# A second seven-product level inside some products of a token-mixing MLP, with the operand sums of g parked in DRAM

## Chip, cores, metric

One core of a Trainium2 chip. The metric is device microseconds (us) of one launch, the median over repeated runs. "Faster" and "slower" mean a difference of over 2%; anything nearer is called "same", with an interval given.

Names: PE is TensorE (PEld its weight loads), DVE is VectorE, ACT is ScalarE, POOL is GpSimd, SP is SyncE, which issues most DMAs here. In the code, p1 to p7 are the seven products of a pair, i1 to i7 those of an inner product, and to park a sum is to write it to DRAM for later.

## The reference, cut to what matters

```python
S, D, F = 2048, 1024, 3584
h  = x + linear_attention(layernorm(x), wqkv, wo)      # 32 heads
u  = gelu(einsum("bsd,sf->bdf", layernorm(h), w1) + b1)   # mixer 1: contracts S
y  = einsum("bdf,fs->bds", u, w2) + b2                    # mixer 2: contracts F
h2 = h + y.transpose                                      # the output, bf16
```

The attention half ends at about 235 us of the 578 us and the change leaves it as it is. The argument is about the two mixers: 2048 x 3584 x 1024 multiply-adds each.

## The kernel before

Both mixers already use one level of a seven-product scheme (Winograd's form of Strassen's). The left operand of a product (w1 or w2) is split into four blocks a11 to a22, the moving operand (h, or g = gelu(u)) into even and odd 128-row tiles (E, O) and left and right 512-column halves. Seven block products replace eight. The price is sums of operands on DVE, and results that are chained through PSUM: B starts as a copy of A after product 1, C as a copy of B after product 6.

One "pair" is two 128-row tiles of the result. A product of a pair is 8 matmuls of 512 columns in mixer 1, 14 in mixer 2:

```python
def mm(self, m, ps, start, ks=None, cols=slice(0, CW)):          # CW = 512
    lhs, mv = self.lhs[m], self.mov[m]
    for k in range(self.nk) if ks is None else ks:               # nk = 8 or 14
        nc.tensor.matmul(ps[:, cols], lhsT=lhs[:, k, :], rhs=mv(k)[:, cols], ...)

def p1(self):  self.mm(1, self.A, True);   nc.scalar.copy(self.B[:], self.A[:])     # cut
def p6(self):  self.mm(6, self.B, False);  nc.scalar.copy(self.C[:], self.B[:])     # cut

def run_pair(st, nxt, pending, cut=None):       # cut: the case without a pending pair
    st.p1(); pending.p4(); st.p5()
    nxt.asum(5)                                 # sums of w blocks for the next pair, on DVE
    st.p6(); nxt.asum(6)
    st.p2(); st.p7(cut); nxt.asum(7)
    st.p3(); nxt.asum(3)

for p in range(NFP):                            # 14 pairs of mixer 1; mixer 2 has 8
    if p + 3 < NFP:
        load_w1_pair(p + 3)                     # w1 is loaded three pairs ahead
    ...
    run_pair(cur, nxt, pend)
```

The sums of g that mixer 2 needs as moving operands (T2, T3 and T4, 14 tiles of 128 x 512 each) stay in SBUF in this kernel.

Of the kernel before, what the change touches and what calls it, by code (L numbers as in the profile page):

```python
# [8 lines left out]
P = 128  # L9
F32 = mybir.dt.float32  # L10
# [10 lines left out]
BANK = 512  # L21
# [6 lines left out]
def kernel(  # L28
# [55 lines left out]
    warm = const.tile([P, BANK], BF16)  # L84
# [41 lines left out]

    w1_tiles = {}
    w2_tiles = {}

    def load_w1_pair(p):  # L130
        w1p = w1pool.tile([P, NS, 2 * P], BF16, tag="w1p", name="w1p")
        nc.sync.dma_start(
            w1p[:],
            B_w1[:, p * 2 * P:(p + 1) * 2 * P].rearrange("(k p) f -> p k f", p=P),
        )
        w1_tiles[p] = w1p

    def load_w2_pair(p, pool):
        w2p = pool.tile([P, NF, 2 * P], BF16, tag="w2p", name="w2p")
        nc.sync.dma_start(  # L140
            w2p[:],
            B_w2[:, p * 2 * P:(p + 1) * 2 * P].rearrange("(k p) s -> p k s", p=P),
        )
        w2_tiles[p] = w2p

    def combine(e, o, t2, t3, t4):
        lo, hi = slice(0, CW), slice(CW, 2 * CW)
        sub = ALU.subtract
        nc.vector.tensor_tensor(t3, o[:, hi], e[:, hi], sub)
        nc.vector.tensor_tensor(e[:, hi], e[:, hi], e[:, lo], sub)  # L150
        nc.vector.tensor_tensor(t2, o[:, hi], e[:, hi], sub)
        if t4 is not None:
            nc.vector.tensor_tensor(t4, o[:, lo], t2, sub)
# [26 lines left out]

    class Product7:
        def __init__(self, wt, nk, mov):
            self.nk, self.mov = nk, mov
            v = wt[:].rearrange("p (k two) (h f) -> p k two h f", two=2, h=2)
            self.a11 = v[:, :, 0, 0, :]
            self.a12 = v[:, :, 1, 0, :]
            self.a21 = v[:, :, 0, 1, :]
            self.a22 = v[:, :, 1, 1, :]
            self.lhs = {1: self.a11, 2: self.a12, 4: self.a22}

        def asum(self, m):
            a, b, op = {
                5: (self.a21, self.a22, ALU.add),
                6: (self.lhs.get(5), self.a11, ALU.subtract),
                7: (self.a11, self.a21, ALU.subtract),
                3: (self.a12, self.lhs.get(6), ALU.subtract),
            }[m]
            t = sapool.tile([P, max(NSP, NFP), P], FP16, tag="sa", name="sa")[:, 0:self.nk, :]
            self.lhs[m] = t
            return nc.vector.tensor_tensor(t, a, b, op)  # L200

        def asums(self):
            return [self.asum(m) for m in (5, 6, 7, 3)]
# [15 lines left out]

        def p1(self):  # L220
            self.A = psw.tile([P, BANK], F32, tag="w", name="psA1")
            self.mm(1, self.A, True)
            self.B = psx.tile([P, BANK], F32, tag="x", name="psB1")
            nc.scalar.copy(self.B[:], self.A[:])

        def p5(self, ks=None):
            if ks is None or ks[0] == 0:
                self.E = psz.tile([P, BANK], F32, tag="z", name="psE1")
            self.mm(5, self.E, True, ks)
            if self.whole(ks):  # L230
                self.shared(self.E)

        def p6(self):
            self.mm(6, self.B, False)
            self.C = psy.tile([P, BANK], F32, tag="y", name="psC1")
            nc.scalar.copy(self.C[:], self.B[:])
# [18 lines left out]
        def p4(self):  # L255
            for a, b, ps in self.parts:
                self.mm(4, ps, False, cols=slice(a, b))
                self.evac(1, 0, ps, a, b)
            self.done()

    class Mixer1(Product7):
        def __init__(self, p):
            super().__init__(w1_tiles[p], NSP, hmov)
            self.p = p

        def shared(self, ps):
            self.e = cpool.tile([P, BANK], F32, tag="e0", name="e1")
            nc.scalar.copy(self.e[:], ps[:])
# [13 lines left out]
        def done(self):  # L282
            p = self.p
            combine(gE[:, p, :], gO[:, p, :], gT2[:, p, :], gT3[:, p, :], None)

    class Mixer2(Product7):
        def __init__(self, p):
            super().__init__(w2_tiles[p], NFP, gmov)
            self.p = p

        def prefetch(self):
            self.hr, self.ot = [], []
            for a in range(2):
                self.hr.append(outp.tile([P, D], BF16, tag=f"hr{a}", name=f"hr{a}"))
                nc.sync.dma_start(self.hr[a][:], h_dram[2 * self.p + a][:])
                self.ot.append(outp.tile([P, D], BF16, tag=f"ot{a}", name=f"ot{a}"))

        def shared(self, ps):
            self.e = []
            for sh in range(2):  # L300
                self.e.append(cpool.tile([P, BANK], F32, tag=f"e{sh}", name="e2"))
                nc.vector.tensor_tensor(self.e[sh][:], ps[:], self.hr[sh][:, CW:D], ALU.add)

        def out(self, sh, c, src, res):
            i = 2 * self.p + sh
            nc.vector.scalar_tensor_tensor(self.ot[sh][:, c], src, b2_sb[:, i:i + 1], res, ALU.add, ALU.add)
            nc.sync.dma_start(o_dram[i * P:(i + 1) * P, c], self.ot[sh][:, c])

        def evac(self, sh, dh, ps, a=0, b=CW):
            c = slice(dh * CW + a, dh * CW + b)  # L310
            self.out(sh, c, ps[:, a:b], self.hr[sh][:, c])

        def evac_shared(self, sh, ps):
            self.out(sh, slice(CW, D), ps[:], self.e[sh][:])

        def done(self):
            pass

# [12 lines left out]
    def run_pair(st, nxt, pending, cut=None):  # L331
        st.p1()
        if pending is None:
            head, last = list(range(st.nk - 1)), [st.nk - 1]
            for ks in (head, last):
                st.p5(ks)
                st.p2(ks)
        else:
            pending.p4()
            st.p5()  # L340
        if nxt is not None:
            nxt.asum(5)
        st.p6()
        if nxt is not None:
            nxt.asum(6)
        if pending is not None:
            st.p2()
        st.p7(cut)
        if nxt is not None:
            nxt.asum(7)  # L350
        st.p3()
        if nxt is not None:
            nxt.asum(3)

    with ExitStack() as actx:
# [516 lines left out]
        sapool = sactx.enter_context(tc.tile_pool(name="sapool", bufs=5, side="right"))  # L872
        w1pool = mctx.enter_context(tc.tile_pool(name="w1pool", bufs=3, side="right"))
# [9 lines left out]
        with ExitStack() as a3:  # L883
# [86 lines left out]
            for (u, j) in q_units[8:]:  # L970
                q_unit(u, j)
                if u >= 1 and j % 2 == 1:
                    i = (u - 1) * TPC + j // 2
                    attn(i)
                    if i % 2 == 1 and i // 2 < 5:
                        (load_wo if i // 2 < 2 else load_w1_pair)((0, 1, 0, 1, 2)[i // 2])
# [33 lines left out]
    gT3 = gpool.tile([P, NFP, CW], FP16, name="gT3")  # L1010
    gT2 = gpool.tile([P, NFP, CW], FP16, name="gT2")
    cpool = ctx.enter_context(tc.tile_pool(name="cpool", bufs=1))
    w2a = ctx.enter_context(tc.tile_pool(name="w2a", bufs=1))
    hmov.update(moving(hE, hO, hT2, hT3, hT4))
    pend = None
    for p in range(NFP):
        if p + 3 < NFP:
            load_w1_pair(p + 3)
        if p == NFP - 3:
            load_w2_pair(0, w2a)  # L1020
        nxt = Mixer1(p + 1) if p + 1 < NFP else Mixer2(0)
        run_pair(cur, nxt, pend)
        pend = cur
        cur = nxt
    pend.p4()
    mctx.close()

    w2b = ctx.enter_context(tc.tile_pool(name="w2b", bufs=2, side="right", reuse_waits="tile"))
    t4pool = ctx.enter_context(tc.tile_pool(name="t4pool", bufs=1, side="right", reuse_waits="tile"))
    outp = ctx.enter_context(tc.tile_pool(name="outp", bufs=2, side="right", reuse_waits="tile"))  # L1030
    load_w2_pair(1, w2b)
    load_w2_pair(2, w2b)
    gT4 = t4pool.tile([P, NFP, CW], FP16, name="gT4")
    half = NFP // 2
    for sl in (slice(0, half), slice(half, NFP)):
        nc.vector.tensor_tensor(gT4[:, sl, :], gO[:, sl, 0:CW], gT2[:, sl, :], ALU.subtract)
    gmov.update(moving(gE, gO, gT2, gT3, gT4))
    pend = None
    for p in range(NSP):
        if p + 3 < NSP:  # L1040
            load_w2_pair(p + 3, w2a if (p + 3) % 3 == 0 else w2b)
        nxt = Mixer2(p + 1) if p + 1 < NSP else None
        cur.prefetch()
        run_pair(cur, nxt, pend, None if nxt is not None else CW - P)
        pend = cur
        cur = nxt
    pend.p4()
# [30 lines left out]
```

## Time and profile before

| | before |
|---|---|
| time, median of 4 runs | 578.89 us (578.86 to 580.63) |
| span of the profiled run | 577.5 us |
| mixer 1 / mixer 2, by the timeline | 235.4 to 405.2 / 405.2 to 574.6 us |

The page of the kernel before (span; busy time of each engine and its share; granted clock in tenths in 40 slices; DMA volume; the chain of work that ended last):

```profile
span 577.5 us, 7392 instructions
...
PE 570.2 (99%) x2832; PEld 267.5 (46%) x2854; DVE 323.6 (56%) x641; ACT 234.0 (41%) x470; POOL 1.8 (0%) x8
...
PEclk9999999999999999999999999999999999999999
...
DMA packets 109827, 66.55 MB, mean 115 GB/s; under 512 B 31826, under 2 KB 101728, under 8 KB 109792
...
PE 94%; DMA 2%; ACT 2%; DVE 2%; issue 1%; SPq 0%; ACTq 0%
```

The windows of the kernel before, one in mixer 1 and two around the turn to mixer 2 (busy us of each engine with the count of instructions, then granted clock, DMA share, GB/s):

```profile
core 0: us, PE busy (x) PEld busy (x) DVE busy (x) ACT busy (x) POOL busy (x), PEclk, DMA share, GB/s
310.00:335.00 25.00, 25.00 (x117) 11.37 (x116) 10.48 (x18) 9.49 (x15) 0.00 (x0) 1.00 0.31 84
406.00:434.00 28.00, 28.00 (x131) 12.70 (x130) 15.17 (x18) 1.79 (x4) 0.00 (x0) 1.00 0.86 229
434.00:460.00 26.00, 26.00 (x122) 11.76 (x121) 10.56 (x13) 1.71 (x3) 0.00 (x0) 1.00 0.59 159
```

PE is busy for the whole of each window at full clock, so the mixers take exactly as long as their matmuls: a pair of mixer 1 takes 12.08 us (its 56 matmuls start 216 ns apart), a pair of mixer 2 takes 21.15 us. DVE and ACT have more than half of each window free. Such a kernel gains only from fewer streamed columns, and it loses one for one whatever makes PE wait.

**A measure.** "Stalls" are worked out from the trace from 228 us on: the time between the starts of two consecutive matmuls, less N/2.4 + 2.5 ns for N columns, counted where it is over 60 ns. The formula is from the Trainium skill, "TensorE: Matmul & The Clock Gate", section Back-to-back issue gap, and this trace agrees with it: 216 ns between 512-column matmuls. The profile's own "idle before" column is smaller (0.19 where the starts show 0.35), because matmul ends are modelled. The trace of the kernel before lacks some matmul records (2832 for 2854 weight loads), and one of them falls after 228 us: at 228.88 a weight load stands without its matmul, in a gap of just one matmul. This 0.2 us is left out, so that the kernel before stalls for 0.4 us in all.

### The profile page before, as it was taken

The numbers are of one execution on the slowest core, as the hardware profiler recorded it, in microseconds if no ns is written. First come the engines' busy times: TensorE is split into PE (matmuls) and PEld (weight loads), VectorE is DVE, ScalarE is ACT, GpSimd is POOL, SyncE is SP. The second block draws the span as 40 slices with busy tenths as digits, with TensorE's granted clock in tenths as the row PEclk, the third lists the DMA queues.
The fourth block names the chain that finished last, engine by engine and source line by source line (L and its number), as shares of the span: only waits on it lengthen the run. The fifth ranks groups of instructions, "written<-read, shape, count | busy, mean of one in ns | idle before, by whom it ended". The sixth has DMA issues, their size and how long they took to land.

```text
span 577.5 us, 7392 instructions
## 1 busy us (share of the span) xinstructions
PE 570.2 (99%) x2832; PEld 267.5 (46%) x2854; DVE 323.6 (56%) x641; ACT 234.0 (41%) x470; POOL 1.8 (0%) x8
## 2 busy tenths in 40 slices
PE   8999999999999999999999999999999999999998
PEld 3444444455555444444444444444444444444444
DVE  6898887556676889654443543435544344343422
ACT  4747777756668766433333333333100000000000
POOL 1000000000000000000000000000000000000000
PEclk9999999999999999999999999999999999999999
DMA  9934321139339952122342223400955634643101
GB/s 302 353 74 83 86 70 37 20 125 266 65 73 183 273 165 92 54 74 73 98 121 74 73 74 88 126 5 1 248 178 149 163 109 128 175 119 109 36 28 36
DMA packets 109827, 66.55 MB, mean 115 GB/s; under 512 B 31826, under 2 KB 101728, under 8 KB 109792
## 3 DMA queue, kind: packets, MB, share of 16 engines
q1 hardware_dynamic: 109056, 65.42, 42.7%
q10 hardware_dynamic: 672, 0.66, 0.3%
q8 instruction: 22, 0.36, 0.3%
q14 instruction: 13, 0.11, 0.1%
q0 software_dynamic: 64, 0.01, 0.0%
HBM read 50.34 MB, written 8.39 MB: 102 GB/s over the span
## 4 chain that ended last, share of the span: by engine, by line
PE 94%; DMA 2%; ACT 2%; DVE 2%; issue 1%; SPq 0%; ACTq 0%
PE acc_t L937 10%; PE acc_t L790 9%; PE psB L521 4%; PE psC L521 4%; PE psA L521 4%; PE psE L521 2%; PE nd_ps L888 1%; DMA xr<-in_A_x_dram 1%; PE psC_4189 L208 1%; PE psB_5038 L208 1%; PE psA_5023 L208 1%; PE psC_4961 L208 1%; PE psC_4831 L208 1%; PE psB_4778 L208 1%; PE psB_4648 L208 1%; PE psA_4633 L208 1%
## 5 line engine op out<-in xcount | busy, mean ns | idle before, releaser
L208 PEld LDWEIGHTS <-sa 128*128 128x128 f16 x896 | 87.7, 98 | 106.0 <-issue 0.4
L790 PE MATMUL acc_t<-xnT,wq_sb 128*128 128x512 bf16 x248 | 57.3, 379 | 0.4
L937 PE MATMUL acc_t<-wo_sb,pqT 128*128 128x512 bf16 x250 | 55.7, 379 | 0.3
L208 PEld LDWEIGHTS <-w2p 128*128 128x128 bf16 x350 | 33.7, 98 | 39.1
L208 PEld LDWEIGHTS <-w1p 128*128 128x128 bf16 x336 | 32.9, 98 | 39.8 <-issue 0.2
L937 PEld LDWEIGHTS <-pqT 128*128 128x128 bf16 x256 | 24.8, 98 | 29.0
L790 PEld LDWEIGHTS <-wq_sb 128*128 128x128 bf16 x256 | 24.5, 98 | 27.4
L160 ACT ACTIVATE e_sb<-acc_t 128x512 bf16<-128x512 f32 x40 | 23.9, 597 | 26.6 <-PE acc_t L790 23.7
L164 DVE TENSOR_SCALAR e_sb<-e_sb 128x512 bf16<-128x512 bf16 x64 | 18.5, 289 | 25.9 <-ACT e_sb L160 25.4
L521 PEld LDWEIGHTS <-xs 128*128 128x128 f16 x208 | 20.0, 98 | 23.4 <-DVE xs L507 1.3
L200 DVE TENSOR_TENSOR sa<-w1p 128x1024 f16<-128x1024 bf16 x28 | 19.1, 684 | 13.7 <-PE psB_2920 L208 1.2
L521 PE MATMUL psA<-wkv,xnT 128*128 128x512 bf16 x98 | 26.4, 379 | 0.3
L948 DVE BATCH_NORM_STATS2 hst<-acc_t 128x6 f32<-128x512 f32 x32 | 22.1, 692 | 6.9 <-ACT h_bf L947 6.5
L200 DVE TENSOR_TENSOR sa<-sa,w1p 128x1024 f16<-128x1024 f16 x14 | 9.7, 691 | 26.8 <-PE psE_3602 L208 2.4
L935 ACT CAST acc_t<-xr 128x512 f32<-128x512 bf16 x32 | 19.0, 593 | 13.5 <-DVE hst L948 13.4
L521 PEld LDWEIGHTS <-xnT 128*128 128x128 bf16 x156 | 15.2, 98 | 18.5 <-issue 0.2
L161 ACT ACTIVATE r_sb<-acc_t 128x512 bf16<-128x512 f32 x40 | 23.7, 593 | 0.0
L200 DVE TENSOR_TENSOR sa<-w2p 128x1792 f16<-128x1792 bf16 x16 | 17.4, 1088 | 9.8 <-DMA w2p<-in_B_w_dram 3.0
L909 DVE TENSOR_TENSOR o_sb<-nd_ps,rd 128x384 bf16<-128x384 f32 (+1 forms) x48 | 21.7, 504 | 1.0 <-ACT rd L904 0.8
L445 PE MATMUL acc_t<-wkv,xnT 128*128 128x512 bf16 x94 | 21.1, 379 | 0.9 <-ACT xnT L698 0.8
L414 DVE BATCH_NORM_STATS2 st<-x_sb 128x6 f32<-128x512 bf16 x32 | 20.4, 681 | 1.6 <-DMA x_sb<-in_A_x_dram 1.6
L947 ACT CAST h_bf<-acc_t 128x512 bf16<-128x512 f32 x32 | 18.3, 574 | 1.2 <-PE acc_t L937 1.1
(506 smaller groups left out, 877.6 us busy)
## 6 DMA issues: line engine op xcount, KB each, us to landing
w1p<-in_B_w_dram SPq DMA_DIRECT2D x14, 1024.0 KB, 5.6
w2p<-in_B_w_dram SPq DMA_DIRECT2D x8, 1792.0 KB, 8.1
xr<-in_A_x_dram SPq DMA_DIRECT2D x16, 256.0 KB, 3.5
x_sb<-in_A_x_dram SPq DMA_DIRECT2D x15, 256.0 KB, 3.1
wkv<-in_A_wqkv_dram SPq DMA_DIRECT2D x2, 1024.0 KB, 9.1
wq_sb<-in_A_wqkv_dram SPq DMA_DIRECT2D x2, 1024.0 KB, 12.7
wo_sb<-in_A_wo_dram SPq DMA_DIRECT2D x2, 1024.0 KB, 6.4
wkv<-in_A_wqkv_dram SPq DMA_DIRECT2D x3, 512.0 KB, 7.0
```

Source lines behind the costliest of these rows:

```text
L160: pin(nc.scalar.activation(e_sb[:], src, ACT.Exp))
L161: pin(nc.scalar.activation(r_sb[:], src, ACT.Relu))
L200: return nc.vector.tensor_tensor(t, a, b, op)
L208: nc.tensor.matmul(ps[:, cols], lhsT=lhs[:, k, :], rhs=mv(k)[:, cols], start=(start and k == 0), stop=(k == self.nk - 1), skip_group_check ...
L414: return nc.vector.bn_stats(st[:, c, :], x_sb[:, c * CW:(c + 1) * CW])
L445: mm = nc.tensor.matmul(pp[:, 0:CW], lhsT=xnT[:, kt, i * P:(i + 1) * P], rhs=wkv[:, kt, c * CW:(c + 1) * CW], start=(kt == 0), stop=(kt == ...
L521: pin(nc.tensor.matmul(ps[:], lhsT=lhs[:, k, :], rhs=rhs[:, k, :], start=(start and k == 0), stop=(k == hk2 - 1), skip_group_check=True,))
L790: nc.tensor.matmul(qp[:, 0:SW], lhsT=wq_sb[:, kt, j * P:(j + 1) * P], rhs=xnT[:, kt, u * SW:(u + 1) * SW], start=(kt == 0), stop=(kt == ND ...
L909: nc.vector.tensor_tensor(o_sb[:, b * JPB * P:(b * JPB + nsl) * P].rearrange("p (s h e) -> p s h e", h=HB, e=DH), blk[:, :, 0:P].rearrange ...
L935: nc.scalar.copy(ap_[:, 0:CW], xr[:, dc * CW:(dc + 1) * CW])
L937: nc.tensor.matmul(ap_[:, 0:CW], lhsT=pqT[:, j, i * P:(i + 1) * P], rhs=wo_sb[:, j, dc * CW:(dc + 1) * CW], start=(j == 0 and not SEED_RES ...
L948: nc.vector.bn_stats(st[:, dc, :], ap_[:, 0:CW])
```

## The change

Intent: use the seven-product scheme a second time inside some of the seven products. Two pairs become a "quad"; the two pairs' product 1 (and, separately, product 5) together form one bigger product, which is again cut into seven. In mixer 1 products 1 and 5 of six of the seven quads are treated so (12 inner products); in mixer 2 product 5 of three of its four (3 inner products). An inner product has 28 matmuls of 256 columns in place of 16 of 512 (mixer 1), or 49 in place of 28 (mixer 2). Its operands, the inner sums and the wider w tiles need SBUF, so T2, T3 and T4 of g no longer stay: they are written to DRAM as they are made and streamed back for every mixer-2 product that needs T3 or T4.

The diff, cut to its core:

```diff
+    class Inner:                                # one inner product of a quad
+        def sums(self):                         # four more sums of w blocks, 128x512 in mixer 1
+            nc.vector.tensor_tensor(sm[0], self.a21, self.a22, ALU.add)
+            ...
+        def i1(self):
+            self.mm(1, self.a, True)            # nk/2 matmuls of 256 columns
+            nc.scalar.copy(self.b, self.a)
+        def i6(self):
+            self.mm(6, self.b, False)
+            nc.scalar.copy(self.c, self.b)
+        ... # i2, i5, i7, i3, i4: results go to the outer A, B or e by ACT copies and DVE adds
+
+    class Quad:
+        def pre(self, m):                       # operand sums for the next quad
+            if m == 5 and self.mov1 is not None:
+                self.in1.sums()
+            for st in self.sts:
+                st.asum(m)
+            if m == 5:
+                self.in5.sums()
+        def run(self, pend, nxt, ...):
+            def interleave(n, fs):              # halves of outer products between dependent steps
+                x = halves(fs)
+                for f in (n.i1, x[0], n.i6, n.i2, x[1], n.i5, n.i7, x[2], n.i3, x[3], n.i4):
+                    f()
+            interleave(self.in1, [st.p4 for st in pend])
+            on_p4()                             # issues the w1 loads of the next quad
+            interleave(self.in5, [st.p6 for st in self.sts])
+            pre(5); ...p2...; pre(6); ...p7...; on_p7(); pre(7); ...p3...; pre(3)
     class Mixer1(Product7):
         def done(self):
-            combine(gE[:, p, :], gO[:, p, :], gT2[:, p, :], gT3[:, p, :], None)
+            sg = stg.tile([P, 3, CW], FP16, tag="sg", name="sg")
+            combine(gE[:, p, :], gO[:, p, :], sg[:, 0, :], sg[:, 1, :], sg[:, 2, :])
+            nc.sync.dma_start(g_park[0][:, p, :, :], sg[:])
...
-    for p in range(NFP):
-        if p + 3 < NFP:
-            load_w1_pair(p + 3)                 # per pair, three pairs ahead
+    def next_load1(u):                          # per quad, in two halves of the contraction,
+        load_w1(u, 0); load_w1(u, 1)            # one quad ahead, into two buffers
...
+    def stream(m, t):                           # T3 before product 7, T4 before product 4
+        nc.sync.dma_start(ts[0][:], g_park[0][:, 0:H2, t, :])
+        nc.sync.dma_start(ts[1][:, 0:NK - H2, :], g_park[0][:, H2:NK, t, :])
+        nc.sync.dma_start(ts[1][:, NK - H2:H2, :], g_park[1][:, :, t, :])
```

## The prediction

> What bounds the kernel now. The page's busy table has PE at 570.2 of 577.5 us, the chain of waits is 94% PE, the granted clock 1.0. DVE (56%), ACT (41%) and DMA (43% of 16 engines) have slack on average. From 235 us on PE never waits: in the timeline a mixer-1 pair (7 products x 8 matmuls of 512 columns) takes 12.08 us, a mixer-2 pair (7 x 14) 21.1 us, so 216 ns per matmul; each mixer costs 169 us. Only fewer streamed columns can help.
>
> What it removes. An inner product replaces 16 matmuls of 512 columns by 28 of 256 (mixer 1), or 28 by 49 (mixer 2). The timeline shows eight 132-column matmuls with eight weight loads passing in 0.48 us, 60 ns each; between that and 216 ns at 512 I estimate 109 ns at 256, the 98 ns weight load (groups by line) just hidden. The Trainium skill (TensorE: Matmul & The Clock Gate, Back-to-back issue gap) gives N/2.4 + 2.5 ns, the same. A mixer-1 inner product saves 16 x 216 - 28 x 109 = 0.40 us, 12 of them 4.8 us; a mixer-2 one 0.70 us, 3 of them 2.1 us. Gross gain 6.9 us, 1.2%: over 2% is out of reach.
>
> What it adds.
> - DVE: inner sums, half-width sinks, T4 sums; some 17 us per 22.5 us mixer-1 quad. Not a bound on average, but the inner chain (0.44 us products, 0.4 us copies, 0.2 us latencies) has only 0.86 us fillers between its steps. I expect 0.1 to 0.3 us of PE wait per inner product, 2 to 3 us in all, and 1 to 3 us once at the first quad, where DVE has two extra sums of 2.8 us.
> - DMA: the parked sums add 5.5 MB of writes and some 20 MB of reads. A mixer-2 quad needs 7.3 MB in 41 us, 177 GB/s; the windows show 290 to 340 GB/s when the queue is full. Sustainable.
> - The turn from mixer 1 to mixer 2 is not. Once the h tiles come free, T2, 12/14 of T3, three w2 tiles of 1.8 MB, h rows and the first T4 must land, about 12 MB: 37 to 40 us in one queue, while the first p4 wants T4 about 28 us after that start. The T4 load can't start before the first p7 ends, and w2 tiles not yet needed stand ahead of it. In strict order PE would idle 4 us before the first p7 and 5 to 9 us before the first p4; if the scheduler fills with p3, p5, p6, p2, it loses 2 to 5 us. I count 5.
>
> Sum: 578.9 - 6.9 + 2.5 + 1.5 + 5 = about 581; I say 580. The gain is real but mostly eaten. Range 573 to 590; faster by over 2% 0.02, within 2% 0.85, slower 0.13.
>
> What would show it. PE work down 7 us, 256-column matmuls 107 to 112 ns apart; windows of a mixer-1 quad 22.5 to 23 us instead of 24.15; PE waits on ACT copies into inner accumulators; a DMA share near 1 for some 35 us at the turn, with PE waiting for streamed T3 or T4; little DMA waiting in later mixer-2 quads.
>
> What would make it wrong. Up: weight loads every 109 ns not quite hidden; DVE, held by a late w1 load, reaching PE every quad; an idle PE losing its clock at the turn. Down: the scheduler placing T4 ahead of the later w2 tiles, or filling so well that the turn costs nothing (572).

## The result

| | before | after |
|---|---|---|
| median | 578.89 us | 582.49 us (581.77 to 583.21, 4 runs) |
| ratio to before, 95% interval | | 1.0055 (1.0032 to 1.0077), "same" |
| span of the profiled run | 577.5 | 580.8 |
| stalls from 228 us on | 0.4 | 10.5 |
| span less stalls | 577.1 | 570.3 |

A ratio, here and below, is the mean time of one kernel's fast runs over the mean of the other's fast runs of the same rounds, so it is not quite the ratio of the medians quoted.

The last two rows of the table are the result in short: 6.8 us of PE work went, as predicted, and 10.1 us of new waiting came.

The page of the kernel after:

```profile
span 580.8 us, 8190 instructions
...
PE 568.5 (98%) x3061; PEld 287.2 (49%) x3061; DVE 363.0 (63%) x755; ACT 252.5 (43%) x547; POOL 1.8 (0%) x8
...
PEclk9999999999999999999999999999999999999999
...
DMA packets 119784, 91.52 MB, mean 158 GB/s; under 512 B 32818, under 2 KB 112192, under 8 KB 119744
...
PE 73%; DMA 10%; DVE 9%; ACT 4%; issue 2%; SPq 0%; ACTq 0%; DVEq 0%
```

The PE share of the span fell by one point only, but the chain of waits says far more: DMA and DVE now hold 19% of it, from 4%. The windows of the kernel after, the same stretches as before:

```profile
core 0: us, PE busy (x) PEld busy (x) DVE busy (x) ACT busy (x) POOL busy (x), PEclk, DMA share, GB/s
310.00:335.00 25.00, 24.50 (x144) 13.84 (x142) 15.23 (x35) 11.53 (x27) 0.00 (x0) 1.00 0.35 116
406.00:434.00 28.00, 27.29 (x128) 12.27 (x127) 18.59 (x25) 3.57 (x6) 0.00 (x0) 1.00 0.94 245
434.00:460.00 26.00, 23.99 (x113) 10.88 (x112) 13.13 (x18) 1.96 (x4) 0.00 (x0) 1.00 0.91 282
```

In mixer 1 half a microsecond of the 25 us is now idle by the busy count, nearly 1 us of a quad by the starts; at the turn it is 2.7 us in 54. DVE is busier by half but still free for 10 us in 25, so no count of busy time explains the waits. They stand in four places:

| place | stall, us | before |
|---|---|---|
| start of mixer 1 (235 to 245 us) | 1.6 | 0.4 |
| first quad (262 to 267) | 1.4 | 0 |
| the five other mixer-1 quads (282 to 388) | 3.9 | 0 |
| the turn to mixer 2 (414 to 458) | 3.6 | 0 |

**A mixer-1 quad, read line by line.** PE of the kernel after as a quad begins at 306.04 (start, length, engine, line, operation, out<-in, shapes, count, and in brackets the idle time before and what ended it):

```profile
306.04 0.60 PE L218 MATMUL psI_3566<-hE,wq 128*128 128x256 f16 x4
306.48 1.03 PE L285 MATMUL psC_3435<-hT_2232,wq 128*128 128x512 f16 x4
307.69 0.60 PE L218 MATMUL psI_3567<-hi_2916,is 128*128 128x256 f16 x4 [0.19 <-ACT psI_3567 L228]
308.12 0.60 PE L218 MATMUL psI_3566<-hE,wq 128*128 128x256 f16 x4
308.56 1.03 PE L285 MATMUL psC_3435<-hT_2232,wq 128*128 128x512 f16 x4
309.77 0.60 PE L218 MATMUL psI_3566<-hE,is 128*128 128x256 f16 x4 [0.19 <-ACT psA_3562 L419]
```

From 306.04 to 306.48, and from 308.12 to 308.56, four 256-column matmuls take 0.44 us, some 109 ns each by the unrounded starts, so the inner products run as fast as hoped. But i6 at 307.69 waits for the ACT copy of i1's result. Why was that copy late? ACT of the kernel after, same place:

```profile
304.23 0.72 ACT L355 ACTIVATE gO<-t_3518,b_sb 128x512 f16<-128x512 f32 x1 [4.21 <-DVE t_3518 L362]
306.04 0.72 ACT L355 ACTIVATE gO<-t_3529,b_sb 128x512 f16<-128x512 f32 x1 [1.08 <-DVE t_3529 L362]
306.66 0.71 ACT L355 ACTIVATE gE<-t_3544,b_sb 128x512 f16<-128x512 f32 x1
307.27 0.36 ACT L228 COPY psI_3567<-psI_3566 128x256 f32<-128x256 f32 x1
```

The copy stands behind gelus of the quad before, and the first of those had waited 4.21 us for a DVE add (t_3518). DVE of the kernel after:

```profile
294.58 0.42 DVE L431 TENSOR_TENSOR e_3408<-psI_3411,es 128x256 f32<-128x256 f32 x1 [0.81 <-PE psI_3411 L218]
298.41 0.43 DVE L210 TENSOR_TENSOR is<-wq 128x512 f16<-128x512 bf16 x1 [3.41 <-DMA wq<-in_B_w_dram]
...
303.18 0.42 DVE L213 TENSOR_TENSOR is<-sa,is 128x512 f16<-128x512 f16 x1
303.51 0.69 DVE L362 TENSOR_TENSOR t_3518<-psC_3435,e_3408 128x512 f32<-128x512 f32 x1
```

DVE waited 3.41 us for the next quad's w1, then did twelve sums in 5.1 us, and only then the add that the gelus wanted. And when w1 was issued, from SP's queue, in the kernel after:

```profile
286.93 0.32 SPq L370 DMA_DIRECT2D g_park_2908<-sg  x1
288.79 0.38 SPq L140 DMA_DIRECT2D wq<-in_B_w_dram  x1
289.97 0.32 SPq L370 DMA_DIRECT2D g_park_2908<-sg  x1
290.34 0.43 SPq L140 DMA_DIRECT2D wq<-in_B_w_dram  x1
```

The first half of w1 leaves only 6.3 us into the quad that begins at 282.52, after SP's queue has waited for PE to end the last product that uses the tile. The second half leaves behind a park store, and that store had to wait for the last T4 sum on DVE, which ended at about 289.9; this costs at most 1.2 us (289.17 to 290.34). The chain is therefore: the load waits for a free tile and then for a store, DVE waits for load, gelu waits for DVE, copy waits for gelu, PE waits for copy. With its 0.9 us of stall this quad takes 24.3 us (from 306.04 to 330.31), where two pairs took 24.16 before: the two inner products of a quad gain nothing while the chain stands.

**The turn.** PE of the kernel after:

```profile
419.73 1.67 PE L285 MATMUL psC_4610<-gs_4500,sa 128*128 128x512 f16 x7 [0.71 <-ACT psC_4610 L321]
...
446.69 1.67 PE L285 MATMUL psC_4755<-gs_4703,sa 128*128 128x512 f16 x7 [0.54 <-DMA gs_4703<-g_park_2908]
...
450.03 1.67 PE L285 MATMUL psC_4755<-gs_4704,sa 128*128 128x512 f16 x7 [0.80 <-DMA gs_4704<-g_park_2908]
```

and its SP queue:

```profile
413.11 0.33 SPq L1262 DMA_DIRECT2D g_park_2909<-sg  x1
413.49 0.42 SPq L1261 DMA_DIRECT2D g_park_2909<-gs_4501  x1
414.01 0.41 SPq L147 DMA_DIRECT2D wq<-in_B_w_dram  x1
...
418.41 8.01 SPq L147 DMA_DIRECT2D wq<-in_B_w_dram  x2
426.46 6.64 SPq L388 DMA_DIRECT2D out_dram<-ot  x2
433.20 0.40 SPq L1241 DMA_DIRECT2D gs_4633<-g_park_2908  x1
```

w2 of the next pair leaves at 414.01, behind stores that wait for the last sums of g (one of them for 4.3 us, from 408.8 to 413.11), and the DMA share is only 0.17 from 410 to 415 us. T4 leaves at 433.20. The two output stores before it, 6.64 us, were not waiting for DVE: the first alone took 6.14 us to be issued, and the output sums of that time had ended at 416.79 and 424.50. The last w2 load had taken 7.54 us to be issued as well, and the DMA engines were full (the columns are those of the windows above):

```profile
425.00:430.00 5.00, 5.00 (x25) 2.26 (x24) 4.86 (x6) 0.57 (x1) 0.00 (x0) 1.00 1.20 291
```

The share (it can pass 1 by the profile's count) is 1.11 to 1.20 in each 5 us window from 415 to 435 us. So three w2 tiles of 1.8 MB stood ahead of T4, that of pair 3 among them, which is needed only in the second quad. (That full engines slowed the issue is the likely reading; the trace names no cause for those 6.14 us.) Later, at 458 to 540 us, the mixer-2 quads run without a stall, one quad in 41.61 us (from 458.74 to 500.35) against 42.3 for two pairs before.

### The profile page after: what moved, and what is told of

It is laid out like the page before. It is cut to its first block, busy times and chain, and to the rows that moved or that the text cites. A ratio compares the mean times of both kernels' runs of the same rounds, so it can differ in the third digit from the quotient of the medians.

```text
span 580.8 us, 8190 instructions
## 1 busy us (share of the span) xinstructions
PE 568.5 (98%) x3061; PEld 287.2 (49%) x3061; DVE 363.0 (63%) x755; ACT 252.5 (43%) x547; POOL 1.8 (0%) x8
## 2 busy tenths in 40 slices
DMA packets 119784, 91.52 MB, mean 158 GB/s; under 512 B 32818, under 2 KB 112192, under 8 KB 119744
## 4 chain that ended last, share of the span: by engine, by line
PE 73%; DMA 10%; DVE 9%; ACT 4%; issue 2%; SPq 0%; ACTq 0%; DVEq 0%
PE acc_t L963 9%; PE acc_t L1111 9%; DMA wq<-in_B_w_dram 6%; PE psB L694 4%; PE psC L694 4%; PE psA L694 4%; DVE sa L277 2%; PE psE L694 2%; PE nd_ps L1062 1%; DMA xr<-in_A_x_dram 1%; PE psC_4610 L285 1%; DMA gs_4633<-g_park_2908 1%; ACT gO L355 1%; PE psB_4544 L285 1%; PE psA_5495 L285 1%
## 5 line engine op out<-in xcount | busy, mean ns | idle before, releaser
L285 PEld LDWEIGHTS <-sa 128*128 128x128 f16 x716 | 70.0, 98 | 80.1 <-issue 3.8
L285 PEld LDWEIGHTS <-wq 128*128 128x128 bf16 x590 | 57.2, 98 | 63.0 <-issue 2.5
L277 DVE TENSOR_TENSOR sa<-wq 128x1024 f16<-128x1024 bf16 (+1 forms) x44 | 36.1, 829 | 19.6 <-DMA wq<-in_B_w_dram 14.9
L166 ACT ACTIVATE e_sb<-acc_t 128x512 bf16<-128x512 f32 x40 | 23.9, 597 | 26.6 <-PE acc_t L963 24.3
L218 PEld LDWEIGHTS <-is 128*128 128x128 f16 x276 | 26.9, 97 | 16.9 <-issue 6.3
L277 DVE TENSOR_TENSOR sa<-wq,sa 128x1024 f16<-128x1024 bf16 (+1 forms) x22 | 18.3, 830 | 10.4 <-PE psI_4907 L218 3.1
L277 DVE TENSOR_TENSOR sa<-sa,wq 128x1024 f16<-128x1024 f16 (+1 forms) x22 | 18.2, 829 | 0.0
```

What stands on the lines that cost most here:

```text
L166: pin(nc.scalar.activation(e_sb[:], src, ACT.Exp))
L218: nc.tensor.matmul(ps, lhsT=self.lhs[m][:, k, :], rhs=self.mov[m][:, k, :], start=(start and k == 0), stop=(k == self.nk - 1), skip_group_ ...
L277: return nc.vector.tensor_tensor(t, a, b, op)
```

## The experiments

My theory after this reading: the gross gain is whole; the stalls come (a) from the late w1 load through DVE's order, (b) at the turn from w2, T3 and T4, (c) at the start and in the first quad from DVE's extra moving sums and too few filler products. Rivals: that the inner chain itself (PE to ACT to PE) costs the stalls whatever the load does; that the turn is short of bandwidth rather than badly ordered; that the gross gain is smaller than it looks.

Stalls by place, in us, and the span of the profiled run less the stalls, which is what PE would need without any wait:

| kernel | median | start | first quad | other quads | turn | span less stalls |
|---|---|---|---|---|---|---|
| before | 578.89 | 0.4 | 0 | 0 | 0 | 577.1 |
| after | 582.49 | 1.6 | 1.4 | 3.9 | 3.6 | 570.3 |
| e1 | 579.65 | 1.6 | 1.4 | 0.7 | 3.3 | 570.5 |
| e2 | 583.13 | 1.6 | 1.4 | 4.0 | 3.5 | 570.3 |
| e3 | 579.92 | 1.6 | 1.4 | 4.0 | 0.9 | 570.2 |
| e4 | 581.39 | 0.9 | 0 | 0 | 4.3 | 574.9 |
| e5 | 582.41 | 1.6 | 1.4 | 4.3 | 3.1 | 570.3 |
| e6 | 582.25 | 1.6 | 1.4 | 4.4 | 2.5 | 569.9 |
| e7 | 581.93 | 1.6 | 1.4 | 4.4 | 1.9 | 570.1 |
| e8 | 581.68 | 1.6 | 0.7 | 3.9 | 2.5 | 570.3 |
| e10 | 580.45 | 1.6 | 1.4 | 4.0 | 0.9 | 570.4 |
| e12 | 576.01 | 0.9 | 0.7 | 0.7 | 0.9 | 571.0 |

The last column is the check on the whole account: it stays within 569.9 to 571.0 for every kernel with all 15 inner products, though their spans differ by 6.7 us. The turn's entry varies from 2.5 to 4.3 us among kernels whose turn is unaltered (after, e1, e4, e5, e8), presumably since it depends on the moment at which the turn is reached; single entries of that column are worth no more than that. e9 and e11 are left out here, because a slowed clock enters their stalls.

### e1: mixer 1 without its w1 loads (wrong)

```diff
+        if u >= 2:                       # every later quad uses the tile that is there
+            w1_tiles[u] = w1_tiles[1]
+            return
         if half == 0:
             w1_tiles[u] = w_tile(...)
```

> Wrong result on purpose: from the third quad on, mixer 1 reuses the second w1 tile and loads nothing. Reference: after 582.5 us; its PE stalls at the first inner product of the quads at 307, 331, 356, 380 us are 0.91, 1.03, 1.03, 0.84 us, that at 283 us 0.14. Theory (late w1: the 2 MB w1 load lands 9.6 us after its issue, DVE, which runs in order, waits 3.4 us for it and then does 5 us of sums before the adds of p7; the gelus come late and collide with the inner copies): these four stalls drop to about 0.15 each, 3.1 us gained, 579.4. Rival (the inner chain itself is too short for ACT and DVE whatever the load does): the stalls stay, 582 to 582.5.

Measured: 579.65 us, ratio 1.0013 (0.9994 to 1.0032); result wrong (relative error 0.021). The four stalls of 0.8 to 1.0 us fell to 0.14 each. The inner chain itself therefore costs 0.14 us per quad, and the late load does the rest: about 3.2 us. The rival that the chain costs it whatever the load does, falls.

### e2: w2 of pairs 1 to 3 issued before the last sums of g

```diff
     bind(7, ts)
+    load_w2(1, wpool)
+    for p in (2, 3):
+        load_w2(p, w2b)
     cur = Mixer2(0)
     ...
-    load_w2(1, wpool)
-    for p in (2, 3):
-        load_w2(p, w2b)
```

> Right result. Three w2 loads are put before the four last sums and the parking of the last two pairs. Theory A (bytes: what must land at the turn takes longer than PE has work for): the order of the loads changes little, at most 1 us, turn stalls stay near 3.6 us. Theory B (in after, the w2 loads stand in SP's queue behind parking stores that wait for DVE until 413 us, so the DMA engines idle some 5 us at 408 to 414, and T4 comes late for that): turn stalls fall to 0 to 1.5 us, 2 to 3.6 us gained, 579 to 580.5.

Measured: 583.13 us, ratio 1.0082 (1.0055 to 1.0109); correct. A miss: the stall moved and did not shrink. The second T4 sum had only one buffer, waited for the store of the first one, and so the second half of T4 left at 437 us; one stall of 2.1 us took the place of several smaller ones. The DMA share was 0.50 and 0.42 in the 5 us windows from 430 on, so the transfers had room there: the queue was held, not full. Two of the six runs were longer, 587.18 and 584.26 us at granted clocks of 0.994 and 0.997; no trace of them was kept, so it is not known whether the wait of 2.1 us cost them the clock.

### e3: mixer 2 without the streamed T3 and T4 (wrong)

```diff
-    load_t3, load_t4 = stream(7, 1), stream(4, 2)
+    load_t3, load_t4 = nop, lambda: bind(4, ts)     # T3's first tiles serve for all
```

> Wrong result on purpose: T3 is loaded once and used for T4 too, no streaming in mixer 2. Both theories of the turn (bytes or queue order of the streamed T3 and T4) expect its six stalls (3.6 us) to go, 579 us, and nothing else to change. If the turn's stalls have another cause (sums, h rows, PSUM), they stay and the time stays above 581.5.

Measured: 579.92 us, ratio 1.001 (0.9996 to 1.0025). It computes the wrong thing by intent, though its error stayed within the tolerance of the comparison (so "correct" in this document means within that tolerance, and no more). The turn lost all but 0.88 us of its stall: product 7 waiting for the ACT copy of C (the line at 419.73 above), which no stream touches. Between these two traces streaming costs 2.7 us, at the turn alone, and the medians differ by 2.6 us.

### e4: mixer 1 without inner products, mixer 2 as changed

```diff
-        return Quad([Mixer1(2 * u), Mixer1(2 * u + 1)], mov1, mov5)
+        return Quad([Mixer1(2 * u), Mixer1(2 * u + 1)], None, None)
-    pend = run_pair(cur, pend, nxt, after1=sums1, after5=sums5)
+    pend = run_pair(cur, pend, nxt)
```

> Right result. Mixer 1 without inner products, everything else as in after (quads, parking, wide w1 loads, mixer 2 with its inner product). The inner products of mixer 1 take 4.8 us off PE's work, but their stretch also shows about 6.5 us of PE stalls that before did not have (1.2 at the start, 1.4 at the first quad, 3.9 later). If all those stalls belong to the inner products and their sums: 4.8 us more work, 6.5 us less stall, 580.8. If the stalls come from the wide, late w1 loads or the parking: they stay or are hidden only in part, 584 to 587.

Measured: 581.39 us, ratio 1.0034 (1.0018 to 1.005); correct. No stall between 244 and 417 us. Its span less stalls is 574.9, so the 12 inner products of mixer 1 are worth 574.9 - 570.3 = 4.6 us and the three of mixer 2 577.1 - 574.9 = 2.2 us. As the change builds them, those of mixer 1 seem to cost some 1 us net, since this kernel's median is 1.1 us under that of the one after; the intervals of the two ratios overlap, so this is not shown beyond noise. The start stall fell too, to 0.9, which was a hint that a moving sum causes it.

### e5: the next quad's sums spread over DVE's free stretches

```diff
-            pre(5)                        # ...then pre(6), pre(7), pre(3)
+            later(0)                      # sums of inner product 1
             for st in self.sts: st.p2()
             ...p7...
+            later(1)                      # sums of product 5, tied behind the p7 adds
             ...p3...
+            later(2)                      # sums of inner product 5 and product 6, tied likewise
                                           # later(3): the rest, in the next quad
```

> Right result. In the mixer-1 quads the next quad's sums are split and pinned: only the four sums of the next inner product 1 (1.4 us) may stand before the adds of p7 and p3; the two asums of product 5 come after the p7 adds, the inner sums of product 5 and the asums of product 6 after the p3 adds, those of 7 and 3 in the next quad. The w1 loads stay late. Theory (the late load hurts only because 5 us of sums stand before the adds on DVE): the four stalls of 0.84 to 1.03 us fall to 0.15 to 0.4 each, 2 to 3 us gained on after, 579.5 to 580.5. Rival (the load itself is the limit, the next inner product waits for it directly): stalls stay near 0.9 each or move to the first weight load of the next quad, 582 to 583.

Measured: 582.41 us, ratio 1.0063 (1.005 to 1.0075); correct. A miss. The old stall went but three smaller ones came in each quad (0.41 + 0.19 + 0.25 us), now also in the one that had been clean, because the deferred sums met the adds of inner product 1. On average DVE has room; between the landing of w1 and the start of the next quad it has not. The load has to come earlier.

### e6 and e7: at the turn, w2 early and a second buffer for T4 sums; and w2 of pair 3 last

```diff
-        sg = outp.tile([P, CW], FP16, tag="sg", name="sg")
+        sg = outp.tile([P, CW], FP16, tag="ot", bufs=3, name="sg")    # e6: e2 and this
-    pend = run_pair(cur, [], nxt, on_p7=load_t4)
+    pend = run_pair(cur, [], nxt, on_p7=lambda: (load_t4(), load_w2(3, w2b)))    # e7: e6 and this
```

> Right result. The early w2 loads of e2, plus a second buffer for the parked T4 sum, so that the second parking store no longer waits for the first to land and the second half of T4 is not issued behind it (in e2 the DMA gap only moved from 410 to 415 to 430 to 440 us). Theory B, mended (idle DMA engines from in-order queues, not bytes): the DMA share stays near 1 until T4 has landed at about 432, stalls at the turn fall from 3.5 to 0.9 to 2 us, 580 to 581. Theory A (bytes) or C (T4, T3, T4 follow each other through one buffer, so each reload's 5 us lies bare whenever PE has no filler left): stalls stay near 3.5, 582.5 to 583.

> Right result. As e6, and the w2 load of pair 3, not needed before the second quad, is issued after the first T4 instead of before it. Theory A (bytes ahead of T4 count): 1.8 MB fewer ahead of T4 bring it 6 us earlier, stalls at the turn 0.9 to 1.5 us, 580, better than e6. Theory B: no better than e6. Theory C: stalls shrink only if the scheduler also moves p4 earlier, 581 to 583. A late w2 of pair 3 could make a new wait at the second quad's p1.

Measured: e6 582.25 us, ratio 1.006 (1.0046 to 1.0073); e7 581.93 us, 1.0051 (1.0038 to 1.0063); both correct. Stalls at the turn 2.5 and 1.9 us: e6 lies within the spread of the unaltered turns, so it shows no gain, and e7 is just below it. Neither time can be told from that of the kernel after. Moving w2 of pair 3 let the first half of T4 leave at 421.7, where it left at 428.9 in e6. In e7 the DMA share was 0.26 and 0.61 in the 5 us windows from 425 to 435: half of T4 had left at 421.7, and the other half only at 431.0, behind an output store that waited 8.3 us for DVE. That pointed to the store itself.

### e8: start of mixer 1 and first quad

```diff
+                if name[0] == "h":
+                    pin(i)                # tie the inner moving sums behind earlier DVE work
...
-                hs = [lambda f=f, ks=ks: f(ks) for f in fs for ks in (lo, hi)]
-                return hs + [nop] * (4 - len(hs))
+                n = len(fs) * nk // 4     # four fillers even when one product is pending
+                return [lambda f=f, a=a: f(list(range(a, a + n))) for f in fs for a in range(0, nk, n)]
```

> Right result. The inner moving sums of mixer 1 are pinned to the place where the program has them (in after one of 0.69 us runs at 237.4 us, between the last two normalisations, and the chain of the last normalisation ends 1 us later than in before), and the first quad's one pending p4 is cut in quarters, so that each step of the inner chain has a filler. Theory: the start's 0.9 us wait (p2 for the copy of p1) falls to 0.1 to 0.2 as in before, the first quad's 1.4 us falls to 0.5 to 1.0; 1.2 to 1.6 us gained, 581. If the waits have another cause they stay, 582.5.

Measured: 581.68 us, ratio 1.0048 (1.0035 to 1.006); correct. The first quad's stall halved, from 1.4 to 0.7. The start's didn't move, but the trace says that the edit missed: the first moving sum still ran at 237.3 us, between the last normalisations, so it tested nothing there. e12 does it properly.

### e9: w1 per pair, park stores on the GpSimd queue

```diff
-            w1_tiles[u] = w_tile(...)     # a quad's tile, two halves of the contraction
+        w1_tiles[p] = wbig[0][:, a:a + NS * 2 * P]...   # a pair's tile: free, and loaded, pair by pair
...
-                nc.sync.dma_start(g_park[0][:, p, :, :], sg[:])
+                nc.gpsimd.dma_start(g_park[0][:, p, :, :], sg[:])
```

> Right result. The w1 tile of a quad is loaded per pair (256 columns each, as before had it) instead of per half of the rows, so that the first pair's half can start when the first pending p4 is done, and the parking stores of mixer 1 go to GpSimd's queue, so that the second load no longer stands behind a store that waits for DVE. Theory (DVE waits for the late w1 load, e1): w1 lands 3 to 5 us earlier, DVE waits less than 1 us for it, the four stalls near 0.9 us fall to 0.15 to 0.4, 579.5 to 580.5 as e1. Rival of e5 (DVE has too much work in the quad, however early the load): the stalls stay at 0.6 or more each, 582.

Measured: 602.98 us, ratio 1.0426 (1.0402 to 1.0449), granted clock 0.98; correct. The worst miss, told with e11, which fails in the same way in the quads. e9 also waited 4.2 us for w2 at the turn and lost its clock there; e11, with the turn of e10, did not.

### e10: at the turn, stores on the GpSimd queue

```diff
-        nc.sync.dma_start(g_park[1][:, t, 1, :], ...)     # and T4's
+        nc.gpsimd.dma_start(g_park[1][:, t, 1, :], ...)
...
-            nc.sync.dma_start(o_dram[...], ot[:, a:b])
+            (nc.gpsimd if self.p < NSP - 2 else nc.sync).dma_start(o_dram[...], ot[:, a:b])
```

It stands on e7.

> Right result. As e7, with the parking stores of the last two pairs and the output stores (but the last quad's) on GpSimd's queue instead of SP's. In e7 the second half of T4 was issued 9 us after the first, behind an output store that waited for DVE, and the DMA engines idled at 425 to 432 us. Theory B: without stores in SP's queue T4 is issued at once, PE's waits at the turn fall from e7's 1.85 us to 0.9 to 1.2, 580.5 to 581.5. Theory C (one buffer for T4, T3, T4 in a row): the last two waits (1.0 us) stay. A slower store path on GpSimd could cost at PSUM or at the end.

Measured: 580.45 us, ratio 1.0027 (1.0013 to 1.004); correct. The turn's stall is down to the 0.88 us of e3, with every byte of the stream still moved. Both halves of T4 leave early now, in SP's queue of e10:

```profile
421.38 0.37 SPq L1241 DMA_DIRECT2D gs<-g_park  x1
422.89 0.37 SPq L1242 DMA_DIRECT2D gs<-g_park  x1
```

So the bytes in sum did not cost the 2.7 us; what stood ahead of T4 in SP's queue did. In the kernel after that was mostly w2 of pair 3 and the full engines; once it had been moved (e7), a store that waited for DVE. The step from e7 to e10, which moves the stores alone, is worth 1.0 us of stall; the rest of the 2.7 us belongs to e7's changes together, as far as the spread of that column lets one say. The Trainium skill, "DMA: Bandwidth & Descriptors", section Anatomy of one DMA — SWDGE (gpsimd) path, says that "DMA engines do not wait on semaphores" and that the wait happens on the issuing sequencer; the 8.3 us for which SP's queue waited for DVE in e7, with a DMA share of 0.26 from 425 to 430 us, agree with it.

### e11: all of e8, e9 and e10

> Right result. e8, e9 and e10 together, with w2 of pair 1 pinned behind T2 and T3 in SP's queue. If the stalls add up as three separate causes: after 582.5 less 0.8 (first quad), 2.9 (late w1) and 2.4 (turn) gives 576.4, 0.4 % faster than before. If they share slack, so that what one gives another takes: 577.5 to 580.

Measured: 595.3 us, ratio 1.0266 (1.0238 to 1.0293), granted clock 0.989; correct. The turn was as good as in e10, the mixer-1 quads were far worse. PE of e11 in one quad:

```profile
324.22 1.03 PE L289 MATMUL psB<-hT,sa 128*128 128x512 f16 x4
328.23 1.01 PE L222 MATMUL psI<-hi,sa 128*128 128x256 f16 x4 [2.99 <-DVE e L434]
329.04 3.19 PE L289 MATMUL psA<-hO,wq 128*128 128x512 f16 x7
```

and DVE of e11:

```profile
323.19 0.42 DVE L434 TENSOR_TENSOR e<-psI,es 128x256 f32<-128x256 f32 x1 [1.11 <-ACT es L245]
326.48 0.43 DVE L214 TENSOR_TENSOR is<-wq 128x512 f16<-128x512 bf16 x1 [2.87 <-DMA wq<-in_B_w_dram]
...
327.76 0.42 DVE L434 TENSOR_TENSOR e<-psI,es 128x256 f32<-128x256 f32 x1
```

Each engine's instructions are ordered by a scheduler when the kernel is built; it seems to have taken the load to land sooner than it does, for it put sums that need the new w1 (326.48) between the two adds that end inner product 5 (323.19 and 327.76). DVE works in order, so the second add waited for the DMA, and i4 on PE, which needs its PSUM space, waited for that add. Then a second loss follows: the matmuls after the wait run at half speed, seven of 512 columns in 3.19 us against 1.67 us for seven at the turn above. The windows of e11:

```profile
328.00:334.00 6.00, 5.77 (x16) 2.31 (x16) 3.39 (x9) 1.06 (x2) 0.00 (x0) 0.50 0.01 3
```

A granted clock of 0.50. The theory of this: it is the order, not the early loads. The rival: the loads disturb by themselves.

### e12: e11 with DVE's order fixed

```diff
+            hold = pin if m == 5 and ... else (lambda i: i)
             for st in self.sts:
-                st.asum(m)
+                hold(st.asum(m))         # behind the adds of inner product 5
-                self.in5.sums()
+                self.in5.sums(hold)
...                                       # the first inner moving sum tied to the last normalisation
```

> The last version: everything of e11_all, and the operand sums of the next mixer-1 quad (those that need the newly loaded w1 tile) are tied behind the two adds that finish the current quad's inner product 5, so that they can no longer stand in front of them on VectorE; and the first inner moving sum is tied behind the last normalisation, which e8 meant to do and did not. My theory (e9 and e11 lost because VectorE, which works in order, waited for w1 with those adds behind it, and PE, idle for 2 to 3 us, lost its clock): the 2.3 to 3.5 us stalls go, the granted clock is 1.0 again, w1 lands about 13 us into the quad, in time for the sums, and PE stalls after 228 us are 0.9 (start) + 0.7 (first quad) + 0.15 x 6 + 0.9 (turn), about 3.5 us in place of about 10.3; the time is 575.5 to 577.5, a ratio of 0.994 to 0.998 to the kernel before. Rival 1 (the earlier w1 loads themselves disturb, by DMA load or by where they make buffers come free): stalls of over 1 us per quad stay and it is over 580. Rival 2 (VectorE has no room: with the sums behind the adds the p7 add is late again, as in e5): 0.5 to 0.9 us per quad, 578.5 to 581. If the clock is lost again, over 590.

Measured: 576.01 us (575.38 to 576.46, 5 runs; before in the same rounds 579.04), ratio 0.9944 (0.9931 to 0.9958), clock 1.0, correct: "same" as the kernel before by the 2% rule, but below it by 0.56%, with an interval clear of 1, and by medians 1.1% below the kernel after. All stalls together are 3.1 us. DVE of e12 in one quad, which begins at 305.26:

```profile
316.09 0.42 DVE L436 TENSOR_TENSOR e<-psI,es 128x256 f32<-128x256 f32 x1 [3.41 <-ACT es L247]
317.32 0.42 DVE L436 TENSOR_TENSOR e<-psI,es 128x256 f32<-128x256 f32 x1 [0.81 <-PE psI L224]
319.64 0.42 DVE L216 TENSOR_TENSOR is<-wq 128x512 f16<-128x512 bf16 x1 [1.90 <-DMA wq<-in_B_w_dram]
...
324.86 0.69 DVE L367 TENSOR_TENSOR t<-psC,e 128x512 f32<-128x512 f32 x1
```

Both adds come first, then the sums. w1 is there 14.4 us into the quad (319.64 - 305.26), where the kernel after had it at 15.9 (298.41 - 282.52) in the quad shown above, and the p7 add comes at 19.6 us in place of 21.0. With this shift of 1.4 us the stall of a quad falls from 0.9 us to 0.14. The rival that the early loads disturb falls, and so does the rival that DVE has no room. The start stall went from 1.6 to 0.9 with the moving sum out of the way (the wait for the copy of product 1 from 0.90 to 0.17 us, as in e4, which has no such sum), so that cause is shown, too.

## Why the prediction was right or wrong

The record says 580.0, within 573 to 590, "same" most likely; 582.49 is inside and "same". Its terms, one by one:

| term of the sum | predicted | measured | from |
|---|---|---|---|
| gross gain | 6.9 us | 6.8 (4.6 mixer 1, 2.2 mixer 2) | after, e4 |
| waits in the inner chain and quads | 2 to 3 | 0.7 for the chain, 3.2 for the late w1 load | e1 |
| first quad | 1 to 3 | 1.4 | after |
| start of mixer 1 | not named | 1.2 more than before, 0.7 of it from one sum | after, e12 |
| the turn | 5 | 3.6 (0.9 product 7's copy, 2.7 the stream; unaltered turns spread from 2.5 to 4.3) | e3, e10 |

- **Right: what bounds it and what it can gain.** 256-column matmuls start 109 ns apart and the weight loads hide (98 ns each), so the risk named there did not come. The gross gain was within 0.1 us.
- **Right in kind, wrong in cause: the quads.** "I expect 0.1 to 0.3 us of PE wait per inner product" charges the stall to the chain of products, copies and latencies. e1 shows 0.14 us per quad, or 0.07 per product, for that chain. The stall was the item that the text put under what would make it wrong: "DVE, held by a late w1 load, reaching PE every quad". It should have been in the sum. It could have been read from the diff: the kernel before loads w1 three pairs ahead, the one after one quad ahead into two buffers, so that it waits for a tile to come free, and its second half leaves behind a park store.
- **Wrong by plain arithmetic: "windows of a mixer-1 quad 22.5 to 23 us".** Two inner products save 0.80 us of 24.15, which leaves 23.35; e12 shows 23.52 with a stall of 0.14. Measured after: 24.3.
- **Near in amount, right in part of the reason: the turn.** "The turn from mixer 1 to mixer 2 is not" sustainable, it says: it counts the bytes of one queue and adds that "w2 tiles not yet needed stand ahead of it", of T4. The trace bears this out, with a DMA share of 1.11 to 1.20 from 415 to 435 us and w2 of pair 3 ahead of T4. What it did not see are the stores in the same queue: those of the last sums of g kept w2 back until 414.01, and in e7, with w2 of pair 3 out of the way, an output store that waited for DVE held T4. e10 moves the same bytes in another order and the stall of the stream is gone, so "37 to 40 us in one queue" makes PE wait in this order only. That the scheduler would fill with other products was right, as the kernel after did product 5, 6, 2 and a half of product 3 of the next pair before the first part of product 4.
- **Missed: the start.** No one of the terms covers it. An inner moving sum of 0.7 us, which stands later in the program, ran between the last two normalisations and delayed the ACT copy after product 1.
- **Right: DMA volume** (92 MB predicted by the sum of its parts, 66.55 + 5.5 + 20; 91.52 measured), and no DMA wait in later mixer-2 quads.

With the measured terms the sum closes: 578.9 - 6.8 + 1.2 + 1.4 + 3.9 + 3.6 = 582.2, against 582.49. That the total came so near is in part luck: the quads cost 1.4 us more than counted and the start 1.2 us that nobody counted, while the turn cost 1.4 us less, and the 9.0 us of waiting that were counted became 10.1.

Left open: the 0.88 us at the turn where product 7 waits for the copy of C with nothing to fill; the 0.7 us left in the first quad; and whether the loads by pair or the park stores on another queue brought w1 forward in e12. How much of e12's gain each of its parts brings was not taken apart by runs, only by the stalls at each place.

## What to carry to other kernels

When PE is busy all the time, count what a change removes in streamed columns, then go through every engine's queue in order and ask what each instruction would wait for, with real landing times: a free engine on average says nothing, since one early instruction that waits for a DMA holds everything behind it. Keep stores that wait for compute out of the queue that issues the next loads, and loads that are needed later behind those that are needed first. And when a load is made earlier, look at what the scheduler now places in front of what: e11 took 16 us longer than the kernel before because in four of the quads an add stood behind a sum that waited for a load, after which the clock fell in three of them, and e12 got that back by tying the order down.

## What the Trainium skill lacked or had wrong

- "TensorE: Matmul & The Clock Gate", section Back-to-back issue gap: it calls N/2.4 + 2.5 ns the isolated gap and gives 131 ns per matmul as the sustained figure at N = 512. The traces here sustain 216 ns at 512 columns for over 300 us, and 109 ns at 256, with a weight load for each matmul: here the formula is the sustained figure too.
- The same page, section Part 1, has the clock fall after an idle window of about 3.4 us. In e9 and e11 it fell to 0.50 after waits of 2.25, 3.15, 3.29, 3.32, 3.34, 3.46, 3.47 and 4.21 us, five of the eight shorter than that, for 3.4 or 6.8 us each; in the profiled executions waits of 2.09 us (e2) and 2.36 us (e11) cost nothing. Its remark that the window is free-running fits: in the clock records of e9 and e11 every change of the clock within the kernel lies on one grid of 3.41 us, and each fall comes at the end of a grid window in which PE had been idle for 2.24 us or more. The wait of 2.25 us lay in one window; of the 2.36 us in e11 only 2.08 lay in one, and of the 2.09 us in e2 only 1.55. So a window need not be idle throughout: here 2.24 us of one lost the clock, and 2.08 us did not.
- The same page, specification table, says that ScalarE and VectorE queues are strict FIFO. e11 agrees (the add at 327.76 behind the sum at 326.48), and neither this page nor another that I found says what it costs: 2.2 to 3.5 us of PE time in each of four quads in e9 and e11, and in all but one of these the clock.
- "Trainium Kernel Development and Optimization", section Key Constraints: issuing DMAs from several engines "only saves the sequencer's issue time". e10 shows a second use: stores moved to GpSimd no longer hold up loads in SP's queue. Stalls at the turn fell from 1.9 to 0.9 us and the time from 581.93 to 580.45 us, in separate batches, with the same bytes.
